# A new hand-written order for a fused attention and highway kernel, with fewer SBUF operations on VectorE

## Chip, cores and metric

The kernel runs on one core of a Trainium2 chip. The metric is device time in microseconds (us) of one execution. The engines are TensorE (PE for matmuls, PEld for its weight loads), VectorE (DVE), ScalarE (ACT), GpSimd (POOL), and SyncE (SP), which here only issues transfers (DMA). [...]

## The reference

First decayed linear attention over blocks of 64, for 4 batches, 8 heads, 768 positions and 64 columns per head; then a highway layer on the 3072 x 512 result.

```
intra = (qb @ kb.T) * lam**(i - j) for i >= j;  intra = intra @ vb
out   = intra + (qb * lam**(i + 1)) @ state
state = lam**64 * state + (kb * lam**(63 - j)).T @ vb
H = max(x @ w_h, 0);  T = sigmoid(x @ w_t + b_t);  result = T * H + (1 - T) * x
```

## The kernel before

The work is cut into 12 steps n of 256 positions, three to a batch, each with two halves b of 128 positions. A step loads k, q and v as f32 (256 KB for each half load), casts k and q to bf16 (CK, CQ), scales v by lam to a negative power (CV), transposes k and q on PE (TK, TQ in step 0; RKF, RQF, or RK, RQ in pieces of 64 rows, later) and copies them out of PSUM (EK, EQ, FK, FQ). Then come the scores (S; SA and SB with the state's matmuls laced in), the causal mask (M, DVE), the state k'v kept in PSUM (U) and copied to SBUF (KE), the product of q with the state (I), the product of masked scores with v (A), and the scaling of the result by lam to a positive power (D, DVE), which gives the transposed rows xT of the second layer. These are turned back on PE (TX, TXB) and copied to `xs` (XC).

The second layer has for each half step two FFN blocks F of four matmuls of 512 columns: F.n.b.0 with w_h into bank h, F.n.b.1 with w_t into bank t, which BP has filled with the bias. Then H = max(h, 0) - x (DVE), G = sigmoid(t) (ACT; "@S" writes it to SBUF for POOL), X = G times H (DVE or POOL), Y = X + x (DVE or POOL) and ST, the store. The last half step goes in two pieces of 256 columns (n.b.0 and n.b.1). W are the four loads of the weights (512 KB each), WC their casts.

Set-up: PW.i fills pow_o[:, i], the powers of lam for step i of a batch, with four exponentials on ACT. QB multiplies a column of ones with the bias row so that every partition has it, RB copies it to SBUF. PT loads ACT's table for the sigmoid. Z.r issues r matmuls whose result nobody reads.

The order of everything is written out in PLAN (lines 16 to 70): tokens `name.args@engine=banks`, issued from left to right, each engine working off its own tokens in that order; nothing is reordered. "Lk.0.1" loads the second half of k of step 0; tile names with a ring of buffers (BUFS, line 72) wait until the tenant before has been read. Lines that the profile names: 198 and 194 loads of k, v and q; 202 loads of W; 111 and 113 a copy or cast on ACT and on DVE or POOL; 221 CV; 233 transposes; 262 scores; 267 state; 304 M; 324 I; 335 A; 341 D; 346 PW; 378 F; 387 QB; 391 H; 396 G; 400 X; 404 Y; 408 and 412 stores; 418 Z; 437 PT.

Of the kernel before, what the change touches and what calls it, by code (L numbers as in the profile page):

```python
# [21 lines left out]
Lk.2.1 WC.1.1.0@ACT WC.1.1.1@POOL S.1.0=14 D.0.1@DVE KE.0.1@ACT WC.1.0.1@POOL Lq.3.0 BP.0.1.2@DVE=0 PT F.0.0.1.2
M.1.0.1 Lq.3.1 CV.1.2@POOL M.1.1.1 TXB.0.0=3 G.0.0.2@S F.0.1.1.2 Lk.3.1 M.1.1.0 Z.2=6 M.1.0.0 G.0.1.2@S U.1.0 Lk.3.0
WC.0.1.0@POOL A.1.1=52 BP.1.0.2@DVE=0 KE.1.0@ACT TXB.0.1=4 WC.0.1.1@POOL Lv.2.1 A.1.0 BP.1.1.2@ACT=6 I.1 CQ.2.2@DVE
XC.0.2.1@ACT U.1.1 D.1.0@DVE RQF.2=1 Lv.2.0 WC.0.0.1@ACT WC.0.0.0@POOL F.1.0.1.2 EQ.2.1@DVE XC.0.2.0@ACT D.1.1@DVE
Lv.3.0 EQ.2.0@ACT F.0.1.0.2=4 CK.2.2@DVE Lv.3.1 TXB.1.1=3 TXB.1.0=5 H.0.1.2 Lq.4.0 XC.1.2.1@ACT RKF.2=1 F.0.0.0.2=2
KE.1.1@ACT X.0.1.2@POOL EK.2.1@DVE Lq.4.1 XC.1.2.0@ACT EK.2.0@DVE S.2.0=31 G.1.0.2@S H.0.0.2 Lk.4.0 CQ.3.2@POOL
S.2.1=45 F.1.1.0.2=0 M.2.1.1 Lk.4.1 CK.3.2@ACT Y.0.1.2@POOL M.2.0.1 RQF.3=5 Lv.4.1 M.2.0.0 RKF.3=2 EQ.3.1@ACT M.2.1.0
F.1.0.0.2=4 Lq.5.0 EK.3.1@ACT CV.2.2@POOL H.1.1.2 EK.3.0@ACT S.3.1=31 Lq.5.1 H.1.0.2 EQ.3.0@ACT F.1.1.1.2 M.3.1.1
BP.2.0.2@ACT=0 Lv.4.0 CV.3.2@POOL U.2.0 M.3.0.1 S.3.0=25 Lk.5.0 KE.2.0@ACT A.2.0=14 M.3.0.0 A.2.1 I.2 Lk.5.1  # L30
CQ.4.2@ACT M.3.1.0 X.0.0.2@POOL U.3.0 D.2.0@DVE Lv.5.0 A.3.1=32 G.1.1.2 A.3.0 D.2.1@DVE RQF.4=5 KE.3.0@ACT Lv.5.1
CK.4.2@POOL F.2.0.1.2 EQ.4.0@DVE X.1.1.2@DVE Lk.6.0 I.3 Y.0.0.2@POOL G.2.0.2@S RKF.4=1 EQ.4.1@DVE Lk.6.1 D.3.0@DVE
F.2.0.0.2=4 EK.4.0@ACT D.3.1@DVE Lq.6.0 CQ.5.2@POOL EK.4.1@ACT TX.2.2=56 U.3.1 XC.2.2.0@ACT Lq.6.1 S.4.1=01
Y.1.1.2@DVE CV.4.2@POOL TXB.3.0=3 XC.2.2.1@ACT RQF.5=5 M.4.0.1 Lv.6.1 KE.3.1@ACT TXB.3.1=2 F.3.0.0.2=6 H.2.0.2
XC.3.2.0@ACT Lq.7.1 EQ.5.1@ACT M.4.1.1 CK.5.2@POOL F.2.1.0.2=0 XC.3.2.1@ACT H.3.0.2 Lv.6.0 EQ.5.0@ACT X.1.0.2@POOL
BP.3.0.2@DVE=4 SA.4=3 RKF.5=1 Lq.7.0 KE.4.0@ACT M.4.1.0 F.3.0.1.2 BP.2.1.2@ACT=6 CV.5.2@POOL EK.5.1@DVE Lk.7.0
EK.5.0@ACT H.2.1.2 SB.4=2 G.3.0.2 S.5.1=53 M.4.0.0 Lk.7.1 F.2.1.1.2 BP.3.1.2@ACT=0 M.5.1.1 Y.1.0.2@POOL Lk.8.1
KE.4.1@ACT I.4=12 M.5.0.1 CK.6.2@ACT Lk.8.0 A.4.0 SB.5=3 X.3.0.2@DVE X.2.0.2@POOL SA.5=5 G.2.1.2 A.4.1 Lv.7.0 M.5.1.0
F.3.1.1.2 CQ.6.2@ACT X.2.1.2@DVE Lv.7.1 Y.2.0.2@POOL F.3.1.0.2=5 D.4.0@DVE G.3.1.2@S Lq.9.1 KE.5.0@ACT CV.6.2@POOL
D.4.1@DVE RK.6=46 RQ.6 BP.4.1.2@ACT=0 Lq.8.1 M.5.0.0 F.4.0.0.2=1 FK.6.1@ACT H.3.1.2 Lq.8.0 FK.6.0@ACT TXB.4.0=3  # L40
FQ.6.0@DVE TXB.4.1=2 CQ.7.2@POOL XC.4.2.0@ACT F.4.1.1.2 FQ.6.1@DVE Lk.9.0 XC.4.2.1@DVE H.4.0.2 CK.7.2@POOL S.6.1=46
Lk.9.1 G.4.1.2@S SA.6=3 M.6.0.1 I.5=52 KE.6.0@ACT Y.3.0.2@POOL Lq.9.0 M.6.1.0 A.5.0 BP.4.0.2@ACT=1 SB.6=4 A.5.1
M.6.1.1 KE.6.1@ACT Lv.8.0 Y.2.1.2@POOL RQ.7=03 RK.7 D.5.1@DVE CK.8.2@ACT F.4.0.1.2 Lv.8.1 D.5.0@DVE CV.7.2@POOL
FQ.7.0@ACT TXB.5.1=6 M.6.0.0 Lv.9.1 F.4.1.0.2=2 G.4.0.2 FQ.7.1@DVE Lv.9.0 FK.7.1@ACT XC.5.2.1@DVE TXB.5.0=4
X.4.0.2@DVE RKF.8=5 FK.7.0@ACT X.3.1.2@POOL ST.0 I.6=63 XC.5.2.0@DVE EK.8.1@ACT SA.7=0 H.4.1.2 A.6.1 ST.1 EK.8.0@ACT
A.6.0 CQ.8.2@POOL S.7.1=41 M.7.1.0 KE.7.0@ACT F.5.1.0.2=5 Lq.11.1 D.6.0@DVE BP.5.0.2@ACT=2 CK.9.2@POOL Lq.11.0 RQF.8=0
# [5 lines left out]
D.7.0@DVE SA.9=6 Y.4.1.2@POOL A.8.0 Lv.11.0 BP.7.0.2@ACT=5 D.7.1@DVE F.6.1.1.2 KE.9.0@ACT X.5.1.2@POOL ST.2 M.9.1.0
CQ.10.2@ACT TXB.7.1=4 F.7.0.1.2 D.8.1@DVE ST.4 Y.5.0.2@POOL G.6.1.2@S BP.6.0.2@DVE=3 F.7.1.0.2=6 XC.7.2.1@ACT ST.3
D.8.0@DVE G.7.0.2@S Y.5.1.2@POOL TXB.7.0=4 H.7.1.2 S.9.1=21 CK.11.2@ACT SB.9=5 M.9.0.1 CK.10.2@POOL ST.5 F.6.0.1.2
BP.7.1.2@ACT=0 M.9.1.1 XC.7.2.0@ACT M.9.0.0 RK.11=26 CV.10.2@POOL G.6.0.2@S RQ.11 RQ.10=14 KE.9.1@ACT FQ.11.0@DVE
RK.10 TX.8.2=53 FQ.11.1@DVE FQ.10.1@ACT F.7.1.1.2 FK.11.1@DVE XC.8.2.1@ACT FK.11.0@DVE X.6.0.2@POOL FK.10.1@DVE
# [19 lines left out]
def kernel(  # L76
# [82 lines left out]
    for i in range(1, NST):  # L159
        P.tensor_scalar(off[:, i], in0=off[:, 0], scalar1=float(2 * C * i), scalar2=None, op0=ALU.mult)  # L160
# [183 lines left out]
    def powers(i):  # L344
        for hp in range(NP):
            A.activation(pow_o[:, i, :, hp, :], t_f, AF.Exp, scale=off[:, 0, hp:hp + 1], bias=off[:, i, hp:hp + 1] if i else 0.0)
# [39 lines left out]
    def spread(bk):  # L386
        T.matmul(bank(("qb",), bk[0], [128, DM]), lhsT=ones, rhs=b_row, start=True, stop=True)
# [9 lines left out]

    def gate(n, b, p, eng):
        y = buf("y", n, b)[:, cols(p)]
        ENG[eng].tensor_tensor(y, in0=buf("g", n, b)[:, cols(p)] if eng == "POOL" else get("t", n, b, p), in1=y, op=ALU.mult)  # L400

    def total(n, b, p, eng):
        z = cols(p)
        ENG[eng].tensor_tensor(buf("ob", n)[:, b, z], in0=buf("y", n, b)[:, z], in1=buf("xs", n)[:, b, z], op=ALU.add)  # L404
# [69 lines left out]
```

## Time and profile before

| | |
|---|---|
| runs shown | 103.04 us median of 3 (102.52 to 105.31) |
| the profiled execution | 102.99 us; span from first to last instruction 101.3 us |
| TensorE clock granted, mean | 0.987 |
| read and written | 20.97 MB, 6.29 MB |
| chain that ended last | PE 31%, DMA 29%, SP's issuing 10%, POOL 7%, DVE 7% |

The profile is one execution. A page and views of it give busy time of each engine, for the whole span or for stretches; the chain of work that ended last, followed back from the end; the timeline of an engine; and groups of instructions by line and shape. Matmuls are pipelined and their ends are modelled, so one matmul's duration is longer than the distance to the next.

### The profile page before, as it was taken

How to read it: one execution, taken by the hardware profiler on the slowest of the kernel's cores; microseconds unless marked ns; L12 is line 12 of the kernel's file. 1: busy time of each engine (PE TensorE's matmuls, PEld its weight loads, DVE VectorE, ACT ScalarE, POOL GpSimd, SP SyncE). 2: the span in 40 equal slices, each digit the busy share in tenths (PEclk: the TensorE clock that was granted, in tenths of full speed). 3: DMA queues.
4: the chain of work that ended last, by engine and by line, in shares of the span. 5: the costliest groups of instructions: out<-in, count | busy, mean ns of one | idle time of the engine just before them, and what ended most of it. 6: DMA issues, size and time to landing. Idle time of an engine off the chain costs nothing.

```text
span 101.3 us, 4242 instructions
## 1 busy us (share of the span) xinstructions
PE 91.9 (91%) x1784; PEld 57.0 (56%) x1803; DVE 85.7 (85%) x157; ACT 74.5 (74%) x134; POOL 82.3 (81%) x83
## 2 busy tenths in 40 slices
...
GB/s 22 309 300 311 357 338 365 366 340 302 254 292 306 338 300 290 299 271 304 283 288 288 319 314 395 392 310 279 294 392 364 36 6 201 6 21 366 239 307 112
DMA packets 33335, 27.54 MB, mean 272 GB/s; under 512 B 1443, under 2 KB 26275, under 8 KB 33316
## 3 DMA queue, kind: packets, MB, share of 16 engines
...
q8 instruction: 14, 0.23, 1.0%
...
q10 hardware_dynamic: 4, 0.00, 0.0%
HBM read 20.97 MB, written 6.29 MB: 269 GB/s over the span
## 4 chain that ended last, share of the span: by engine, by line
PE 31%; DMA 29%; SPq 10%; POOL 7%; DVE 7%; issue 7%; ACT 5%; DVEq 0%; POOLq 0%; ACTq 0%
DMA kf<-in_k_dram 14%; PE bt L378 9%; PE bh L378 9%; DMA w_f<-in_moe_w_h_dram 8%; DMA qf<-in_q_dram 7%; SPq L198 5%; SPq L194 4%; PE kv L267 2%; PE bs L262 2%; POOL ob L404 2%; POOL kb L113 2%; DVE y L391 2%; POOL vs L221 2%; PE bo L335 2%; SPq L202 2%
## 5 line engine op out<-in xcount | busy, mean ns | idle before, releaser
L304 DVE TENSOR_TENSOR m<-bs,tri 128x512 bf16<-128x512 f32 x48 | 31.0, 681 | 1.2 <-PE kv L267 1.0
L221 POOL TENSOR_TENSOR vs<-vf,pow_v 128x1024 bf16<-128x1024 f32 (+1 forms) x13 | 23.4, 1805 | 5.1 <-DMA vf<-in_v_dram 3.1
L378 PEld LDWEIGHTS <-xT 128*128 128x128 bf16 x200 | 17.7, 98 | 16.8 <-DVE xT L341 0.3
L404 POOL TENSOR_TENSOR ob<-y,xs 128x512 f32<-128x512 bf16 x21 | 24.3, 1173 | 0.6 <-DVE y L400 0.4
L378 PE MATMUL bh<-w_b,xT 128*128 128x512 bf16 (+1 forms) x93 | 23.8, 370 | 0.5
L378 PE MATMUL bt<-w_b,xT 128*128 128x512 bf16 (+1 forms) x89 | 23.1, 370 | 1.1 <-issue 0.3
L400 POOL TENSOR_TENSOR y<-g,y 128x512 bf16<-128x512 f32 x15 | 17.3, 1159 | 2.7 <-DVE y L391 2.6
L391 DVE SCALAR_TENSOR_TENSOR y<-bh,xs 128x512 bf16<-128x512 f32 (+1 forms) x25 | 16.3, 660 | 1.8 <-PE bh L378 1.8
L341 DVE TENSOR_TENSOR xT<-bo,pow_o 128x512 bf16<-128x512 f32 x24 | 15.6, 679 | 0.1
L111 ACT ACTIVATE ss<-kv 128x512 bf16<-128x512 f32 x19 | 11.4, 601 | 3.9 <-PE kv L267 3.8
L396 ACT ACTIVATE g<-bt 128x512 f32<-128x512 f32 x15 | 9.0, 602 | 5.0 <-PE bt L378 4.4
L111 ACT ACTIVATE bt<-b_bc 128x512 f32<-128x512 f32 (+1 forms) x20 | 11.5, 580 | 1.4 <-DVE xT L341 0.6
L262 PE MATMUL bs<-qT,kT 64*64 64x128 bf16 x384 | 11.5, 220 | 0.0
L111 ACT ACTIVATE xs<-bx 128x512 bf16<-128x512 bf16 x15 | 9.0, 604 | 1.3 <-PE bx L354 0.8
L262 PEld LDWEIGHTS <-kT 64*64 64x64 bf16 x384 | 8.2, 106 | 2.7 <-DVE kT L113 1.2
L267 PE MATMUL kv<-vs,kb 64*64 64x64 bf16 x320 | 8.6, 194 | 0.2 <-POOL vs L221 0.2
L267 PEld LDWEIGHTS <-kb 64*64 64x64 bf16 x320 | 7.0, 109 | 3.0 <-issue 2.0
L335 PE MATMUL bo<-m,vs 64*64 64x128 bf16 x384 | 8.5, 218 | 0.0
L418 PE MATMUL bspin<-blank,id 128*128 128x512 bf16 x26 | 8.3, 444 | 0.1
L113 POOL CAST kb<-kf 128x1024 bf16<-128x1024 f32 (+1 forms) x7 | 6.8, 976 | 1.5 <-DMA kf<-in_k_dram 1.5
L396 ACT ACTIVATE bt<-bt 128x512 f32<-128x512 f32 (+1 forms) x10 | 5.5, 546 | 2.4 <-PE bt L378 2.4
L335 PEld LDWEIGHTS <-vs 64*64 64x64 bf16 x384 | 6.4, 107 | 0.6
...
## 6 DMA issues: line engine op xcount, KB each, us to landing
...
```

What stands on the lines that cost most here:

```text
L111: A.activation(dst, src, AF.Copy)
L221: ENG[eng].tensor_tensor(buf("vs", n)[:, hs], in0=buf("vf", n)[:, hs].rearrange("p h (j d) -> p h j d", j=J), in1=pow_v[:, n % NST, hs, :, ...
L262: T.matmul(get("s", n, e, hp // 2)[half(b), hp % 2, j, :], lhsT=buf("kT", n)[half(e), hp, j, half(b)], rhs=q_cols(n, half(e), hp, b), star ...
L267: T.matmul(kv[half(e), hp, half(e)], lhsT=buf("kb", n)[half(b), j, 2 * hp + e, :], rhs=buf("vs", n)[half(b), 2 * hp + e, j, :], start=firs ...
L304: V.tensor_tensor(buf("m", n, e, u), in0=get("s", n, e, u), in1=tri[:, None].to_broadcast([128, 2, J, C]), op=ALU.mult)
L335: T.matmul(get("o", n, b)[half(e), hp, :], lhsT=buf("vs", n)[half(b), 2 * hp + e, j, :], rhs=buf("m", n, e, hp // 2)[half(b), hp % 2, j, : ...
L341: V.tensor_tensor(cut(buf("xT", n)[:, :, b * C:(b + 1) * C]), in0=get("o", n, b).rearrange("e k (j p) -> e k p j", j=Q), in1=cut(pow_o[:, ...
L378: T.matmul(t, lhsT=buf("xT", n)[:, j, b * C:(b + 1) * C], rhs=w_b[w][:, j, z], start=(j == 0 and not w), stop=(j == KC - 1), skip_group_ch ...
L391: V.scalar_tensor_tensor(buf("y", n, b)[:, z], in0=get("h", n, b, p), scalar=0.0, in1=buf("xs", n)[:, b, z], op0=ALU.max, op1=ALU.subtract)
L396: A.activation(buf("g", n, b)[:, cols(p)] if to == "S" else t, t, AF.Sigmoid)
L400: ENG[eng].tensor_tensor(y, in0=buf("g", n, b)[:, cols(p)] if eng == "POOL" else get("t", n, b, p), in1=y, op=ALU.mult)
L404: ENG[eng].tensor_tensor(buf("ob", n)[:, b, z], in0=buf("y", n, b)[:, z], in1=buf("xs", n)[:, b, z], op=ALU.add)
```

## The change

The order is replaced as a whole. What is different in kind:

- Behind step 0, DVE no longer casts k or q from SBUF to SBUF (CQ.1, CQ.2 and CK.2 were there), and the adds Y.1.1 and Y.8.0 go from DVE to POOL. In step 0, DVE takes over CK.0.0, CV.0.0 and PW.2.
- PW.2 is no longer four exponentials but one product of pow_o[:, 0] with `grown`, the exponential of the per-step offset.
- The bias product QB comes in two halves of 256 columns, QB.0 and QB.1.
- The loads of step 1's v go ahead of the weights, both stand ahead of all of step 2, and v of step 2 goes ahead of q and k of step 3. ST.2 and ST.3 stand among the last loads of v; before, all loads came ahead of ST.2.
- In the last two pieces, t comes ahead of h on PE, and the result is max(h, 0) g + (1 - g) x: G to SBUF, GN = sigmoid(-t) to `rest`, R = rest times x, HG = max(h, 0) times g into `part`, Y = part + rest. R, HG and Y are on DVE.
- Counts by engine: Z 31 matmuls before, 23 after; BP on DVE 5 before, 2 after; X on POOL 15 and 13, Y on POOL 21 and 23.

The head and the end of PLAN, then the functions:

```diff
-Lk.0.0 Lq.0.0 Lq.0.1 Lk.0.1 Lv.0.1 Lq.1.0 Z.9=5 Lq.1.1 PW.0@ACT CQ.0.0@DVE Lv.0.0 CK.0.0@POOL Lk.1.0 Lk.1.1
-CQ.0.1@POOL TK.0.0=2 W.1.0 PW.2@ACT Z.1=5 TQ.0.2=3 CK.0.1@DVE W.1.1 Z.1=5 TK.0.1=4 EQ.0.0@DVE QB=6 EQ.0.1@DVE Lv.1.0
-CV.0.1@POOL EK.0.0@DVE EK.0.1@ACT Lv.1.1 S.0.0=01 RB@ACT S.0.1=53 CQ.1.2@DVE Lq.2.1 Z.3=4 PW.1@ACT M.0.0.0 RQF.1=2
...
-H.10.0.2 G.10.0.2 F.11.0.0.2=1 XC.11.2.0@DVE Y.10.1.2@POOL BP.11.1.1@ACT=6 ST.9 X.10.0.2@DVE F.11.0.1.2 H.11.0.2
-Y.10.0.2@POOL F.11.1.0.0=5 G.11.0.2 TXB.11.1=3 F.11.1.1.0 X.11.0.2@DVE XC.11.2.1@ACT ST.10 F.11.1.0.1=0 G.11.1.0
-H.11.1.0 F.11.1.1.1 Y.11.0.2@POOL H.11.1.1 X.11.1.0@DVE G.11.1.1 X.11.1.1@DVE ST.11.0.2 Y.11.1.0@DVE Y.11.1.1@DVE
-ST.11.1.0 ST.11.1.1
+Lk.0.1 Lq.0.1 Lq.0.0 Lv.0.1 Lk.0.0 Lv.0.0 Z.10=5 CK.0.1@DVE Lq.1.0 PW.0@ACT Lq.1.1 CQ.0.1@POOL Lk.1.0 Lk.1.1
+CQ.0.0@DVE Lv.1.1 PW.1@ACT PW.2@DVE TQ.0.2=2 Lv.1.0 QB.0=3 Z.1=5 EQ.0.0@DVE CV.0.1@POOL W.1.0 CK.0.0@DVE TK.0.1=4
+Z.1=5 EQ.0.1@DVE PT TK.0.0=6 EK.0.1@DVE W.1.1 CV.0.0@DVE S.0.1=01 Z.2=5 W.0.1 M.0.1.1 EK.0.0@ACT U.0.0 W.0.0 S.0.0=24
+CQ.1.2@POOL QB.1 KE.0.0@ACT RB@ACT M.0.1.0 BP.0.1.2@ACT=5 Lq.2.1 U.0.1 M.0.0.0 RQF.1=6 BP.0.0.2@ACT=3 M.0.0.1 I.0=14
+Lq.2.0 CK.1.2@POOL EQ.1.0@ACT A.0.0 KE.0.1@DVE A.0.1 EQ.1.1@ACT Z.1=0 Lk.2.1 D.0.0@DVE RKF.1=2 Z.1=0 Lk.2.0 EK.1.1@ACT
+EK.1.0@DVE Z.1=1 CV.1.2@POOL D.0.1@DVE S.1.0=06 S.1.1=21 TXB.0.1=4 M.1.0.1 Lv.2.1 WC.1.0.0@ACT M.1.1.1 U.1.0
+WC.1.0.1@ACT TXB.0.0=2 M.1.0.0 Z.6=1 M.1.1.0 Lv.2.0 WC.1.1.0@ACT WC.1.1.1@POOL XC.0.2.1@DVE KE.1.0@ACT XC.0.2.0@DVE
+F.0.1.1.2 Lq.3.1 I.1=10 WC.0.1.0@POOL A.1.0 WC.0.1.1@POOL A.1.1 U.1.1 D.1.0@DVE F.0.0.1.2 Lq.3.0 WC.0.0.0@ACT
+WC.0.0.1@POOL D.1.1@DVE G.0.1.2@S TXB.1.0=6 Lk.3.1 KE.1.1@DVE F.0.0.0.2=4 G.0.0.2@S XC.1.2.0@DVE Lk.3.0 CQ.2.2@POOL
...
+D.10.0@DVE F.9.1.1.2 G.8.0.2 X.9.0.2@POOL BP.10.0.2@ACT=2 XC.10.2.1@DVE F.10.1.1.2 M.11.1.1 G.9.1.2 Y.9.0.2@POOL
+X.8.0.2@DVE A.11.1=03 G.10.1.2 A.11.0 X.9.1.2@DVE I.11 Y.8.0.2@POOL F.10.1.0.2=6 BP.11.1.1@ACT=1 D.11.0@DVE
+Y.9.1.2@POOL TXB.10.0=5 ST.8 H.10.1.2 F.10.0.0.2=0 XC.10.2.0@ACT BP.11.0.2@ACT=6 X.10.1.2@DVE F.10.0.1.2 ST.9 H.10.0.2
+Y.10.1.2@POOL F.11.0.0.2=5 D.11.1@DVE G.10.0.2 X.10.0.2@DVE TXB.11.0=4 F.11.0.1.2 XC.11.2.0@ACT BP.11.1.0@DVE=0
+Y.10.0.2@POOL H.11.0.2 TXB.11.1=3 G.11.0.2 F.11.1.1.0 F.11.1.0.0=4 XC.11.2.1@ACT X.11.0.2@DVE ST.10 F.11.1.1.1
+G.11.1.0@S GN.11.1.0 F.11.1.0.1=2 Y.11.0.2@POOL HG.11.1.0 GN.11.1.1 R.11.1.0@DVE G.11.1.1@S R.11.1.1@DVE HG.11.1.1
+ST.11.0.2 Y.11.1.0@DVE Y.11.1.1@DVE ST.11.1.0 ST.11.1.1
...
@@ -158,6 +158,8 @@
         P.tensor_copy(off[half(e), 0], ln[half(e)].rearrange("p (h e) -> p e h", e=2)[:, e])
     for i in range(1, NST):
         P.tensor_scalar(off[:, i], in0=off[:, 0], scalar1=float(2 * C * i), scalar2=None, op0=ALU.mult)
+    grown = singles.tile([128, NST, NP], F32)
+    A.activation(grown[:, 1:], off[:, 1:], AF.Exp)
     pow_o = singles.tile([128, NST, 2, NP, C], F32)
     b_bc = singles.tile([128, DM], F32)
     w_f = [singles.tile([128, KC, DM], F32, name=f"w_f{i}") for i in range(2)]
@@ -173,6 +175,9 @@
     def buf(x, *key):
         return ring[x][turn.get(x, turn["kf"])(*key) % BUFS[x]]
 
+    rest = singles.tile([C, DM], F32)
+    part = singles.tile([C, DM], F32)
+    parted = set()
     made = {}
 
...
-    def powers(i):
+    def powers(i, eng):
+        if eng != "ACT":
+            ENG[eng].tensor_tensor(pow_o[:, i], in0=pow_o[:, 0], in1=grown[:, i, None, :, None].to_broadcast([128, 2, NP, C]), op=ALU.mult)
+            return
         for hp in range(NP):
             A.activation(pow_o[:, i, :, hp, :], t_f, AF.Exp, scale=off[:, 0, hp:hp + 1], bias=off[:, i, hp:hp + 1] if i else 0.0)
 
-    def spread(bk):
-        T.matmul(bank(("qb",), bk[0], [128, DM]), lhsT=ones, rhs=b_row, start=True, stop=True)
+    def spread(p, bk):
+        t = bank(("qb",), bk[0] if bk else 0, [128, DM])
+        T.matmul(t[:, cols(p)], lhsT=ones, rhs=b_row[:, cols(p)], start=p == 0, stop=True, skip_group_check=True)
 
@@ -395,13 +404,27 @@
         t = get("t", n, b, p)
         A.activation(buf("g", n, b)[:, cols(p)] if to == "S" else t, t, AF.Sigmoid)
 
+    def sigm_rest(n, b, p):
+        A.activation(rest[:, cols(p)], get("t", n, b, p), AF.Sigmoid, scale=-1.0)
+
+    def kept(n, b, p, eng):
+        z = cols(p)
+        ENG[eng].tensor_tensor(rest[:, z], in0=rest[:, z], in1=buf("xs", n)[:, b, z], op=ALU.mult)
+
+    def gated(n, b, p):
+        z = cols(p)
+        V.scalar_tensor_tensor(part[:, z], in0=get("h", n, b, p), scalar=0.0, in1=buf("g", n, b)[:, z], op0=ALU.max, op1=ALU.mult)
+        parted.add((n, b, p))
+
     def gate(n, b, p, eng):
         y = buf("y", n, b)[:, cols(p)]
         ENG[eng].tensor_tensor(y, in0=buf("g", n, b)[:, cols(p)] if eng == "POOL" else get("t", n, b, p), in1=y, op=ALU.mult)
 
     def total(n, b, p, eng):
         z = cols(p)
-        ENG[eng].tensor_tensor(buf("ob", n)[:, b, z], in0=buf("y", n, b)[:, z], in1=buf("xs", n)[:, b, z], op=ALU.add)
+        last = (n, b, p) in parted
+        ENG[eng].tensor_tensor(buf("ob", n)[:, b, z], in0=part[:, z] if last else buf("y", n, b)[:, z],
+                               in1=rest[:, z] if last else buf("xs", n)[:, b, z], op=ALU.add)
```

More of the change, by code (lines that the diff above doesn't have):

```diff
@@ L22 @@
[L22 to L46, printed above, removed]
@@ L52 @@
[L52 to L56, printed above, removed]
```

57 lines of the change are left out of this document (39 added, 18 removed).

## The prediction

> **What bounds the kernel now.** I read the page's busy line first, then the view that cuts the span into stretches, then the chain of waits in order of time, then the timeline of each engine at the two ends. Busy times first, then four stretches: before the first useful matmul, to 30.06 us, to 95 us, the rest. The columns of the stretches are length, busy us of PE, PEld, DVE, ACT and POOL, granted clock, DMA share and GB/s.
>
> ```profile
> PE 91.9 (91%) x1784; PEld 57.0 (56%) x1803; DVE 85.7 (85%) x157; ACT 74.5 (74%) x134; POOL 82.3 (81%) x83
> 0.00:6.72 6.72, 5.48 (x15) 2.07 (x16) 2.18 (x6) 4.01 (x9) 4.31 (x18) 1.00 0.64 192
> 6.72:30.06 23.34, 22.24 (x379) 13.67 (x382) 18.69 (x34) 18.18 (x33) 13.48 (x15) 1.00 1.08 327
> 30.06:95.00 64.94, 62.58 (x1380) 40.09 (x1395) 62.02 (x111) 50.86 (x91) 62.69 (x51) 1.00 0.87 266
> 95.00:101.30 6.30, 1.59 (x17) 1.20 (x14) 2.85 (x7) 1.48 (x4) 1.77 (x2) 0.79 0.59 212
> ```
>
> From 30.06 to 95 us PE is idle for only 64.94 - 62.58 = 2.36 us, and what it does there is useful work, because both orders place all idle-filling matmuls (Z) in steps 0 and 1. DVE (62.02) and POOL (62.69) have as little room; ACT has 14 us. So the long middle can give back at most 2.36 us. Before 30.06 it is otherwise: 22.24 us count as busy, but much of that is Z and waiting, and DMA is full (1.08 at 327 GB/s). What an order can win is what PE has finished by 30 us, when data no longer set the pace. The chain shows where PE stands then.
>
> ```profile
> 28.23 0.62 PE bktr L233 x8
> 28.85 0.86 PE bh L378 x4
> 29.72 0.35 PE bs L262 x16
> 30.06 0.97 PE bt L378 x4
> 31.03 0.30 PE kv L267 x12
> 33.08 0.45 PE bo L335 x30
> ```
>
> These are RKF.3, F.1.0, half of S.3, the last FFN block of step 1 (F.1.1.1), U.2 and A.3. They also give my units: F 0.86, U about 0.4, A 0.45, S 0.45. Eight transposes are 0.45: the 0.62 holds the last one's run-out, and F began 0.62 after the first.
>
> **Step by step: the first 30 us.** The arrival of the data decides. Rows of the timeline: start, duration, engine, operation, and in brackets idle time and releaser.
>
> ```profile
> 12.23 1.04 POOL L113 CAST kb<-kf 128x1024 bf16<-128x1024 f32 x1 [0.78 <-DMA kf<-in_k_dram]
> 14.91 1.18 POOL L113 CAST w_b<-w_f 128x512 bf16<-128x512 f32 x2 [0.78 <-DMA w_f<-in_moe_w_t_dram]
> 16.71 1.91 POOL L221 TENSOR_TENSOR vs<-vf,pow_v 128x1024 bf16<-128x1024 f32 x1 [0.62 <-DMA vf<-in_v_dram]
> 21.43 0.62 POOL L113 CAST w_b<-w_f 128x512 bf16<-128x512 f32 x1 [0.94 <-DMA w_f<-in_moe_w_h_dram]
> 23.25 0.69 DVE L113 CAST kb<-kf 128x1024 bf16<-128x1024 f32 x1 [0.36 <-DMA kf<-in_k_dram]
> 27.12 1.06 ACT L111 ACTIVATE kb<-kf 128x1024 bf16<-128x1024 f32 x1 [1.22 <-DMA kf<-in_k_dram]
> 28.82 3.76 POOL L221 TENSOR_TENSOR vs<-vf,pow_v 128x1024 bf16<-128x1024 f32 x2 [0.94 <-DMA vf<-in_v_dram]
> 15.54 1.28 DVE L341 TENSOR_TENSOR xT<-bo,pow_o 128x512 bf16<-128x512 f32 x2
> 16.28 0.82 PE L378 MATMUL bt<-w_b,xT 128*128 128x512 bf16 x3 [0.17 <-DVE xT L341]
> 16.55 1.28 ACT L437 ACT_TABLE_LOAD   x1
> ```
>
> Count SP's loads in pieces of 256 KB (a W is two). The rows tie positions to times: the 10th piece is in at 12.23, the 14th at 14.91, the 16th at 16.71, the 22nd at 21.43, the 24th at 23.25, the 28th at 27.12, the 30th at 28.82: 0.83 us each ((28.82 - 12.23) / 20). The new order of SP gives other tenants: v of step 1 now precedes the weights, so w_t is complete with piece 16 (16.71, not 14.91); w_h with piece 20 (about 20.1, not 21.43); q of step 2 with 22 (21.43), k with 24 (23.25, as before), v of step 2 with 26 (about 25, not 28.82), q of step 3 with 28, k of step 3 with 30 (28.82, not 27.12).
>
> Step 0 in the new order: the costs are these (two rows of the timeline, three of the groups by line with mean ns behind the busy time, one more of the timeline).
>
> ```profile
> 4.41 3.67 ACT L346 ACTIVATE pow_o<-t_f,off 128x256 f32<-128x256 f32 x8
> 4.47 0.42 POOL L160 TENSOR_SCALAR off<-off 128x4 f32<-128x4 f32 x2
> L387 PE MATMUL bqb<-b_row,ones 1*128 1x512 f32 x2 | 1.1, 640 | 0.0
> L304 DVE TENSOR_TENSOR m<-bs,tri 128x512 bf16<-128x512 f32 x48 | 31.0, 681 | 1.2 <-PE kv L267 1.0
> L221 POOL TENSOR_TENSOR vs<-vf,pow_v 128x1024 bf16<-128x1024 f32 x11 | 21.3, 1943 | 2.8 <-DMA vf<-in_v_dram 1.9 <-DVE m L304 0.5 <-DMA qf<-in_q_dram 0.4
> 26.20 2.47 DVE L304 TENSOR_TENSOR m<-bs,tri 128x512 bf16<-128x512 f32 x4
> ```
>
> Four masks take 2.47, so each further full DVE operation costs (2.47 - 0.68) / 3 = 0.60. PW.2 leaves ACT (four of 3.67 / 8 = 0.46, 1.8 us less) for one DVE product of 128x1024. No row shows it: below, a DVE cast of this size is 0.69; above, POOL's two-source product is 1.94. I take 1.2, two masks, the row nearest in kind. CV.0.0 on DVE is likewise one mask, 0.6, between 0.35 (half the cast) and 0.97 (half POOL's product). The exponential `grown` has 8 columns where pow_o has 256 and costs at most its 0.46, but ACT now waits for POOL's `off`, done at 4.89; so PW.0 starts near 5.2 instead of 4.41 and ends at 7.0, PW.1 ends at 8.9, and the table load (1.28), moved here from 16.55, at 10.2. Only then comes EK.0.0, 0.46 or more: S.0.0 starts near 11. DVE meanwhile runs from the arrival of q's second half, the third piece (12.23 - 7 x 0.83 = 6.4): casts and copies of half a step CQ, EQ, CK, EQ, EK at most 0.4 each (a little over half of 0.69), PW.2 1.2, CV 0.6, four masks 2.4, KE 0.6: 6.8, so D.0.0 starts at 13.2, or 13.7 to 14.1 with waits for S.0.0 and for POOL; now it is 15.54. The two bias halves are half of 1.1 each: nothing in sum, only one half moved behind S.0.0.
>
> The gain of 1.5 us in D.0.0 is not kept: the first F needs w_t, in at 16.71, cast by 17.4, so F starts at 17.5 instead of 16.28. From there I add PE's list in units: all eight F, I.1, A.1, U.1, TXB.1, RQF.2, RKF.2, S.2, RQF.3, U.2, A.2. It waits 0.4 for k of step 2 (POOL's or ACT's cast is 1.06) and 0.3 for q of step 3, and reaches RKF.3 at 29.95. At 30.06 the new PE has F.1.1.1 (0.86), U.2 (0.4) and A.2 (0.45) done beyond what it has now, and lacks half of S.3 (0.23) and most of RKF.3 (0.35). **PE is 1.1 us ahead.** Bounds: no gain where v of step 2 comes no sooner than now, and 1.7 if RKF.3 is not late.
>
> **The middle.** From the masks of step 1 on DVE loses two BP and a half, two casts, two adds, and gains two KE and two small copies: by rows 1.6 us less. POOL loses two gates and a cast for two adds, ACT takes three BP, three casts and the like, 4.5 us, of 14 free. Of the copies behind step 0 (CQ.1, CQ.2, CK.2) the last ran at 23.25, when POOL had ended its cast of 21.43 and next had X.0.1, whose H stood behind CK.2 on DVE: it held up nothing. What did collide are the two adds on DVE.
>
> ```profile
> 35.84 1.04 POOL L113 CAST qb<-qf 128x1024 bf16<-128x1024 f32 x1
> 36.59 0.84 DVE L404 TENSOR_TENSOR ob<-y,xs 128x512 f32<-128x512 bf16 x1
> 36.84 2.35 POOL L221 TENSOR_TENSOR vs<-vf,pow_v 128x1024 bf16<-128x1024 f32 x1
> 88.84 1.29 DVE L404 TENSOR_TENSOR ob<-y,xs 128x512 f32<-128x512 bf16 x1
> 89.67 1.49 POOL L404 TENSOR_TENSOR ob<-y,xs 128x512 f32<-128x512 bf16 x1
> ```
>
> The DVE add lasts longer the longer POOL was already at work, and the POOL operation queued behind ends late by 2.35 - 1.94 = 0.41 and 1.49 - 1.15 = 0.34 (the add of the tail's rows): one waits for the other to end. Both adds go to POOL. But PE, not they, is full here, so I credit a quarter of its 2.36 idle: **-0.6**; ends -2.36 (all gone) and +0.8 (a third more idle, from ACT's 4.5 us).
>
> **The tail.** Rows of the timeline from the last gates on.
>
> ```profile
> 95.28 0.69 DVE L400 TENSOR_TENSOR y<-bt,y 128x512 bf16<-128x512 f32 x1 [0.29 <-ACT bt L396]
> 95.32 0.60 ACT L111 ACTIVATE xs<-bx 128x512 bf16<-128x512 bf16 x1
> 95.95 0.76 DVE L391 SCALAR_TENSOR_TENSOR y<-bh,xs 128x256 bf16<-128x256 f32 x2
> 95.99 0.60 PE L378 MATMUL bt<-w_b,xT 128*128 128x256 bf16 x4
> 96.05 1.15 POOL L404 TENSOR_TENSOR ob<-y,xs 128x512 f32<-128x512 bf16 x1 [0.42 <-DVE y L400]
> 96.62 0.83 DVE L400 TENSOR_TENSOR y<-bt,y 128x256 bf16<-128x256 f32 x2
> 96.63 0.37 ACT L396 ACTIVATE bt<-bt 128x256 f32<-128x256 f32 x1 [0.44 <-PE bt L378]
> 97.37 0.75 DVE L404 TENSOR_TENSOR ob<-y,xs 128x256 f32<-128x256 bf16 x2
> ```
>
> DVE is busy without a break from 95.28 to 98.12: X, then six half pieces. New: X, HG, R, R, HG, Y, Y, again six, each 0.36 behind the last and 0.42 long. ACT has four sigmoids of 0.37 for two, behind XC: 95.7, 96.05, 96.4, 96.75 to 97.1. HG.0 runs at 96.1. R reads `rest` and `xs`, both in SBUF, as the colliding adds did, and POOL has Y.11.0 running from 96.05 to 97.2. If R waits for that: R 97.2, R, HG, Y, Y end at 97.2 + 4 x 0.36 + 0.42 = 99.06, **+0.9**. If not, the six end at 96.1 + 5 x 0.36 + 0.42 = 98.3, +0.2. I take +0.9, since both collisions above show such a wait. [...]
>
> **Sum.** The profiled execution took 102.99 us, 1.69 beyond its span of 101.30. 102.99 - 1.1 - 0.6 + 0.9 = **102.2 us**. The median of the runs shown is 103.04, as good as the same, so nothing is added.
>
> **Rivals.**
>
> *Faster: the middle gives too.* DVE and POOL are each 95% busy from 30 us and lose about 1.6 us each, so most of PE's 2.36 idle (say 1.8) may vanish with its cause, the early lead may be 1.5, and R may start ahead of Y.11.0 (tail +0.2): 102.99 - 1.5 - 1.8 + 0.2 = 99.9. For it: the stretches' DVE and POOL columns. Against it: PE's own column, and ACT gets 4.5 us more.
>
> *Slower: the weights come too late.* Place: first F at 17.5, not 16.28. If v of step 2 buys PE nothing, because its F of steps 0 and 1 are still waiting and RQF.3 and RKF.3 (k of step 3 one piece pair later, 1.7 us) become the wait at 30 us, PE is 1.2 to 1.7 us behind instead of 1.1 ahead, and the middle, full, cannot make it up: 102.99 + 1.5 + 0.9 = 105.4. It decides once fewer than seven F are done when RQF.3 starts. For it: DMA is full to 30 us. Against it: the unit count, which has eight.
>
> *The change does not do what it says:* a cast off DVE frees nobody, as at 23.25; then the early lead alone stands against the tail: 102.99 - 1.1 + 0.9 = 102.8, inside the forecast.
>
> **How the numbers follow.** A measurement of this kernel can tell about 2%, 2.1 us, from no change. Forecast with the case that only the early lead counts: 0.54, 101 to 104.5; faster rival 0.29, 99 to 101; slower rival 0.17, 104.5 to 106. The range, from 99.6 to 105.0, leaves about a tenth on each side. Chances: faster by over 2% (below 100.9) 0.29, within 0.55, slower (above 105.1) 0.16.
>
> **What would show it.** The first F near 17.5 and D.0.0 near 14; A.2 done by 30 us; PE idle of under 2 us between 30 and 95; no DVE operation beyond 0.7 us in the middle; R starting when POOL's last add ends, and the last DVE add about 2.5 us behind the last matmul (now 98.12 - 96.59 = 1.5). The prediction is wrong if D.0.0 is later than 15.5, if a load waits long in SP's queue (ST.2 and ST.3 now stand ahead of the last v loads), or if the middle's idle of PE grows beyond 3 us.

## The result and the profile after

| | before | after |
|---|---|---|
| median of 20 runs each | 103.03 us (101.56 to 105.31) | 103.84 us (102.99 to 105.61) |
| ratio (of the runs named below) | | 1.0111, 95% interval 1.0072 to 1.0151 |
| profiled execution, span | 102.99 us, 101.3 us | 104.04 us, 102.3 us |

The new order is slower by about 1%. That is inside the range given and within 2%, but forecast was a small gain. Ratios, here and below, compare only executions that lie within 1.5% of the fastest of their kernel, so they can differ from the quotient of the medians.

The busy line of the page after the change, then the stretches (length, busy us of PE, PEld, DVE, ACT and POOL, granted clock, DMA share, GB/s):

```profile
PE 93.1 (91%) x1801; PEld 57.3 (56%) x1801; DVE 86.1 (84%) x158; ACT 77.1 (75%) x137; POOL 79.1 (77%) x79
6.72:30.06 23.34, 22.08 (x354) 13.31 (x352) 18.84 (x35) 16.86 (x29) 14.38 (x14) 1.00 1.06 350
30.06:95.00 64.94, 63.41 (x1418) 40.16 (x1417) 61.20 (x110) 54.70 (x95) 58.64 (x48) 1.00 0.82 264
95.00:102.30 7.30, 2.11 (x21) 1.67 (x19) 4.15 (x8) 2.19 (x6) 1.94 (x2) 0.82 0.38 144
```

PE's idle time in the middle fell from 2.36 to 64.94 - 63.41 = 1.53 us, DVE (62.02 to 61.20) and POOL (62.69 to 58.64) lost work, as forecast, DVE half of the 1.6 us. The loss shows first at the two ends. First the timeline of the early stage (start, duration, engine, operation, in brackets idle time and releaser):

```profile
14.01 0.68 DVE L346 TENSOR_TENSOR xT<-bo,pow_o 128x512 bf16<-128x512 f32 x1
17.98 1.46 PE L441 MATMUL bspin<-blank,id 128*128 128x512 bf16 x6 [0.21 <-DVE m L309]
19.27 1.03 PE L386 MATMUL bt<-w_b,xT 128*128 128x512 bf16 x4
31.38 0.62 PE L238 MATMUL bktr<-id,kb 128*128 128x128 bf16 x8
```

D.0.0 starts at 14.01, as forecast. But the first F starts at 19.27 and not at 17.5: in front of it in PE's own order stands Z.6, six matmuls whose result nobody reads, into bank 1. (By the plans the order before has 27 such matmuls, not 31, and the new one 23.) That bank frees only when a mask of step 1 has read it, so the six could not fill an idle time; they ran when F could have. RKF.3 comes at 31.38 where 29.95 was forecast.

The end, same view: the last matmul block, POOL's last add, and DVE's last pieces.

```profile
96.51 0.60 PE L386 MATMUL bh<-w_b,xT 128*128 128x256 bf16 x4
96.57 1.15 POOL L426 TENSOR_TENSOR ob<-y,xs 128x512 f32<-128x512 bf16 x1 [0.78 <-DVE y L421]
96.91 1.42 DVE L412 TENSOR_TENSOR rest<-rest,xs 128x256 f32<-128x256 f32 x2
98.26 0.41 DVE L416 SCALAR_TENSOR_TENSOR part<-bh,g 128x256 f32<-128x256 f32 x1
98.59 0.74 DVE L426 TENSOR_TENSOR ob<-part,rest 128x256 f32<-128x256 f32 x2
```

The last matmul ends at 97.11 (96.59 before), the last DVE add at 99.33, 2.22 behind it (1.53 before). From there to the end of the span are about 3.0 us (about 3.2 before). So the span's +1.0 is 0.52 by the last matmul, 0.69 behind it, and about 0.2 given back between the last add and the end.

### The profile page after: what moved, and what is told of

Its sections match the earlier page's. It is cut to its first block, busy times and chain, and to the rows that moved or that the text cites. A ratio compares the mean times of both kernels' runs of the same rounds, so it can differ in the third digit from the quotient of the medians.

```text
span 102.3 us, 4269 instructions
## 1 busy us (share of the span) xinstructions
PE 93.1 (91%) x1801; PEld 57.3 (56%) x1801; DVE 86.1 (84%) x158; ACT 77.1 (75%) x137; POOL 79.1 (77%) x79
## 4 chain that ended last, share of the span: by engine, by line
PE 62%; DVE 21%; ACT 8%; issue 5%; DVEq 0%
PE bt L386 16%; PE bh L386 13%; DVE m L309 7%; PE bspin L441 6%; PE bs L267 6%; PE bo L340 4%; DVE y L400 4%; PE kv L272 3%; PE bo L329 3%; DVE xT L346 2%; PE bx L362 2%; PE bqtr L238 2%; ACT qT L111 2%; ACT kT L111 2%; DVE kT L113 2%
## 5 line engine op out<-in xcount | busy, mean ns | idle before, releaser
L426 POOL TENSOR_TENSOR ob<-y,xs 128x512 f32<-128x512 bf16 x23 | 26.4, 1159 | 3.1 <-DVE y L421 2.9
L386 PE MATMUL bt<-w_b,xT 128*128 128x512 bf16 (+1 forms) x100 | 24.6, 371 | 0.0
L226 POOL TENSOR_TENSOR vs<-vf,pow_v 128x1024 bf16<-128x1024 f32 (+1 forms) x12 | 22.3, 1865 | 2.6 <-DMA vf<-in_v_dram 2.6
L421 POOL TENSOR_TENSOR y<-g,y 128x512 bf16<-128x512 f32 x13 | 15.0, 1161 | 6.8 <-DVE y L400 3.6
L400 DVE SCALAR_TENSOR_TENSOR y<-bh,xs 128x512 bf16<-128x512 f32 x23 | 15.5, 683 | 1.2 <-PE bh L386 1.0
L111 ACT ACTIVATE bt<-b_bc 128x512 f32<-128x512 f32 (+1 forms) x23 | 13.3, 591 | 2.0 <-DVE xT L346 1.1
L267 PE MATMUL bs<-qT,kT 64*64 64x128 bf16 x384 | 12.2, 219 | 1.8 <-ACT w_b L111 0.8
L111 ACT ACTIVATE ss<-kv 128x512 bf16<-128x512 f32 x17 | 10.2, 599 | 2.1 <-PE kv L272 2.0
L405 ACT ACTIVATE g<-bt 128x512 f32<-128x512 f32 (+1 forms) x15 | 8.6, 572 | 2.9 <-PE bt L386 2.6
L267 PEld LDWEIGHTS <-kT 64*64 64x64 bf16 x384 | 8.4, 106 | 3.9 <-DVE kT L113 1.8
L272 PE MATMUL kv<-vs,kb 64*64 64x64 bf16 x320 | 9.1, 194 | 0.0
L272 PEld LDWEIGHTS <-kb 64*64 64x64 bf16 x320 | 7.0, 109 | 2.8 <-issue 2.1
L405 ACT ACTIVATE bt<-bt 128x512 f32<-128x512 f32 x10 | 5.8, 581 | 2.2 <-PE bt L386 2.2
L111 ACT ACTIVATE qb<-qf 128x1024 bf16<-128x1024 f32 x7 | 7.4, 1055 | 0.0
```

Of the source, the lines that this page charges most:

```text
L111: A.activation(dst, src, AF.Copy)
L226: ENG[eng].tensor_tensor(buf("vs", n)[:, hs], in0=buf("vf", n)[:, hs].rearrange("p h (j d) -> p h j d", j=J), in1=pow_v[:, n % NST, hs, :, ...
L267: T.matmul(get("s", n, e, hp // 2)[half(b), hp % 2, j, :], lhsT=buf("kT", n)[half(e), hp, j, half(b)], rhs=q_cols(n, half(e), hp, b), star ...
L272: T.matmul(kv[half(e), hp, half(e)], lhsT=buf("kb", n)[half(b), j, 2 * hp + e, :], rhs=buf("vs", n)[half(b), 2 * hp + e, j, :], start=firs ...
L386: T.matmul(t, lhsT=buf("xT", n)[:, j, b * C:(b + 1) * C], rhs=w_b[w][:, j, z], start=(j == 0 and not w), stop=(j == KC - 1), skip_group_ch ...
L400: V.scalar_tensor_tensor(buf("y", n, b)[:, z], in0=get("h", n, b, p), scalar=0.0, in1=buf("xs", n)[:, b, z], op0=ALU.max, op1=ALU.subtract)
```

## The experiments

Theories before the runs: (Z) the early term is lost to Z.6; (A) the end is longer because R waits for POOL's Y.11.0; (B) the end is longer because of the new form itself, with more operations. A third question came out of the first four runs and is told below.

**Without Z.6.**

```diff
-... M.1.0.0 Z.6=1 M.1.1.0 Lv.2.0 ...
+... M.1.0.0 M.1.1.0 Lv.2.0 ...
```

> The new kernel without the six filling matmuls Z.6 that stand ahead of its first FFN block. Theory A (they are on PE's path: they wait for a mask of step 1 to release their bank, run 17.98 to 19.4 us, and F follows at 19.27 though its weights were cast at 17.5): first F at 17.5 to 17.8 us, PE's last matmul 1.2 to 1.6 us earlier than 97.11, time 1.2 to 1.6 us below the new kernel's 103.84, about 102.4. Rival B (the arrival of q, k of steps 2 and 3 and DVE's masks take the lead back): first F at 17.5 to 17.8, but the last matmul less than 0.4 us earlier, time 103.4 to 103.9. Rival C (PE's clock drops in the gap): the matmuls behind it stand 0.43 us apart instead of 0.215, and the time is above 103.84.

Median 103.61 us (6 runs; before 103.55 on that chip), ratio 1.0016 (0.9927 to 1.0105). Three rows of PE's timeline:

```profile
17.60 1.03 PE L386 MATMUL bt<-w_b,xT 128*128 128x512 bf16 x4
30.07 0.62 PE L238 MATMUL bktr<-id,kb 128*128 128x128 bf16 x8
94.24 0.60 PE L386 MATMUL bh<-w_b,xT 128*128 128x256 bf16 x4
```

F starts at 17.60 and RKF.3 at 30.07: both as forecast, and Z.6 alone cost 31.38 - 30.07 = 1.31 us. The granted clock was 1.00 from 6.72 to 95 us in this profile, so rival C falls. (The profiles below agree, but for those with an early fall of the clock: RKF.3 starts at 29.86 to 30.07 in the seven without Z.6, at 31.38 to 31.63 in the three with it.) In this profile, the shortest of its six executions (101.78 us), the last matmul ends at 94.84, 1.75 ahead of before; the prediction's first two terms were -1.1 and -0.6. That compares a short execution with a middling one of before, whose shortest on this chip took 101.58 us; the medians show no lead.

**More of the same: Z.18 for Z.6.**

```diff
-... M.1.0.0 Z.6=1 M.1.1.0 ...
+... M.1.0.0 Z.18=1 M.1.1.0 ...
```

> The new kernel with eighteen filling matmuls ahead of its first FFN block instead of six (twelve more of 0.215 us: 2.6 us). Theory A (they stand on PE's path and nothing later makes up for a late PE): first F at 21.8 to 21.9 us, the time 2.2 to 2.6 us above the new kernel: 106.0 to 106.5. Rival B (data or DVE's masks set the pace behind them): first F as late, but the time less than 1.0 us above 103.84.

Median 106.56 us (6 runs; before 103.12), ratio 1.0405 (1.0286 to 1.0523). The profile is of an execution in which the clock fell early (two of the six were such); a stretch with that, and two rows of PE:

```profile
15.00:19.00 4.00, 3.70 (x48) 2.16 (x46) 1.17 (x3) 2.39 (x6) 1.56 (x3) 0.55 1.06 392
21.02 4.05 PE L441 MATMUL bspin<-blank,id 128*128 128x512 bf16 x18 [0.21 <-DVE m L309]
24.90 1.03 PE L386 MATMUL bt<-w_b,xT 128*128 128x512 bf16 x4
```

The first F starts 24.90 - 21.02 = 3.88 us behind the first Z (1.29 with six): the fillers stand in the way one for one. The other four runs, at a mean clock of 0.98 or more, took 105.38 to 106.94, on average 2.3 us above after's median, for twelve more fillers of 0.215 us (2.6). So a delay ahead of the first F reaches the end of the kernel.

**The end in the old form.** The last two pieces as before, with t kept ahead of h:

```diff
-G.11.1.0@S GN.11.1.0 F.11.1.0.1=2 Y.11.0.2@POOL HG.11.1.0 GN.11.1.1 R.11.1.0@DVE G.11.1.1@S R.11.1.1@DVE HG.11.1.1
+G.11.1.0 F.11.1.0.1=2 Y.11.0.2@POOL H.11.1.0 X.11.1.0@DVE G.11.1.1 H.11.1.1 X.11.1.1@DVE
```

> The new order, but the last two pieces as before: G times (relu(h) - x), plus x. Theory A (the tail is lengthened because R waits for POOL's add Y.11.0): the last DVE add ends 1.5 to 1.6 us behind the last matmul instead of 2.22, time 0.6 to 0.7 us below the new kernel's 103.84, about 103.2. Rival B (the order of t ahead of h, or ACT, lengthens it): the gap stays above 2.0 us and the time within 0.2 us of 103.84.

Median 104.07 us (6 runs), ratio 1.0143 (1.0066 to 1.0220): no gain in the time. Yet behind the last matmul are 1.76 us instead of 2.22 (and 1.53 where h is ahead of t, below). Timeline, last matmul block and last adds, and one row of the middle:

```profile
97.17 0.60 PE L386 MATMUL bh<-w_b,xT 128*128 128x256 bf16 x4
98.78 0.75 DVE L426 TENSOR_TENSOR ob<-y,xs 128x256 f32<-128x256 bf16 x2
46.65 0.22 PE L272 MATMUL kv<-vs,kb 64*64 64x64 bf16 x2 [1.52 <-issue]
```

What it gained at the end it had lost before the last matmul (97.77 against 97.11), most of it at 46.65: PE stood still for 1.52 us, waiting for nothing that the profile shows ("issue"). This was in none of my theories.

**Both undone.** Without Z.6, and with this old form.

> Both: the new order without Z.6 and with the last two pieces as before. If both theories A hold and add up, 1.8 to 2.3 us below the new kernel: 101.6 to 102.0, that is about 1% faster than the kernel before. If the early lead is taken back (rival B of the first), 103.0 to 103.3, the same as before.

Median 103.53 us (6 runs; before 103.55), ratio 0.9957 (0.9866 to 1.0048). Level with before; span 100.4, one stand-still of 0.45 us at 77.25.

**The new end alone, on the order before.** Only the last two lines of the plan and the functions HG, GN and R.

> The kernel before with only the last two pieces changed: t ahead of h on PE, and relu(h) g + (1 - g) x. Theory A: R waits for POOL's add Y.11.0, the last DVE add 2.2 to 2.5 us behind the last matmul instead of 1.53, time 0.6 to 0.9 us above 103.03: about 103.8. Rival B (no wait, the products only move): within 0.2 us of 103.03.

Median 104.28 us (6 runs), ratio 1.0051 (0.9942 to 1.0160): the time does not settle it. The timeline does:

```profile
98.44 0.60 PE L381 MATMUL bh<-w_b,xT 128*128 128x256 bf16 x4
98.49 1.15 POOL L420 TENSOR_TENSOR ob<-y,xs 128x512 f32<-128x512 bf16 x1 [0.43 <-DVE y L415]
98.98 1.27 DVE L406 TENSOR_TENSOR rest<-rest,xs 128x256 f32<-128x256 f32 x2
100.52 0.74 DVE L420 TENSOR_TENSOR ob<-part,rest 128x256 f32<-128x256 f32 x2
```

Again 100.52 + 0.74 - 99.04 = 2.22 us behind the last matmul, in another order, with the two R beside POOL's add.

**Without POOL's last add.** Y.11.0 is left out.

```diff
-... F.11.1.0.1=2 Y.11.0.2@POOL HG.11.1.0 ...
+... F.11.1.0.1=2 HG.11.1.0 ...
```

> The new kernel without POOL's last add (Y.11.0 is left out, so the half step before the last one is stored unfinished). Theory A (R on DVE waits for this add on POOL to end): the two R take 0.75 to 0.8 us together instead of 1.42, and the last DVE add ends 1.5 to 1.6 us behind the last matmul instead of 2.22. Rival B (R waits for ACT's sigmoids): R takes 1.3 us or more and the gap stays above 2.1 us.

```profile
97.38 0.60 PE L386 MATMUL bh<-w_b,xT 128*128 128x256 bf16 x4
97.78 0.75 DVE L412 TENSOR_TENSOR rest<-rest,xs 128x256 f32<-128x256 f32 x2
98.78 0.75 DVE L426 TENSOR_TENSOR ob<-part,rest 128x256 f32<-128x256 f32 x2
68.38 0.21 PE L267 MATMUL bs<-qT,kT 64*64 64x128 bf16 x1 [1.68 <-issue]
```

The two R take 0.75 instead of 1.42 us, and 1.55 us stand behind the last matmul. Theory A is shown, B falls: the new form is no longer by itself, and no shorter either (1.53 before). Median 102.87 us (12 runs), ratio 1.0049 (0.9990 to 1.0107), again with a stand-still of PE, 1.68 us at 68.38.

**Without Z.6, the end as before** (h ahead of t, too).

> The new order without Z.6 and with the end of the kernel before: h ahead of t on PE, G times (relu(h) - x), plus x. Theory A: first F at 17.6 us, last matmul near 95.2 us, last DVE add 1.5 us behind it, so 1.3 to 1.9 us below the new kernel: 102.0 to 102.5, about 1% faster than the kernel before. Rival B (the middle of the new order is worse than that of before): 102.9 to 103.5.

Median 103.39 us (6 runs; before 103.12), ratio 1.0134 (1.0020 to 1.0248). Behind the last matmul 1.53 us, first F at 17.60: both losses are out, and still it is no faster than before. It has two stand-stills:

```profile
44.97 0.22 PE L271 MATMUL kv<-vs,kb 64*64 64x64 bf16 x2 [1.27 <-issue]
67.30 0.21 PE L266 MATMUL bs<-qT,kT 64*64 64x128 bf16 x1 [0.80 <-issue]
```

**The two colliding adds alone.** Kernel before, with Y.1.1 and Y.8.0 on POOL: the reason that I gave for the middle.

```diff
-Y.1.1.2@DVE ... Y.8.0.2@DVE
+Y.1.1.2@POOL ... Y.8.0.2@POOL
```

> The kernel before with its two adds in the middle, Y.1.1 and Y.8.0, on POOL instead of DVE; nothing else changes. Theory A (the two collisions cost PE nothing, because PE is full): no DVE operation above 0.76 us between 30 and 95 us, and the time within 0.3 us of 103.03. Rival B (the prediction's middle term, -0.6 us, comes from them): 102.2 to 102.6.

Median 103.17 us (6 runs; before 103.12), ratio 1.0112 (1.0013 to 1.0212). No gain, though the collisions are gone (no DVE operation of the middle is above 0.7 us): what they cost DVE and POOL does not reach the end.

**What the stand-stills are.** In several kernels they come in the middle of the laced small matmuls SA.5 (45 us) and SA.8 (67 us), two smaller ones near 78 us, and not in every execution. The page has a DMA queue of the kind "instruction", q8, with 14 packets, 0.23 MB in a run, so about 16 KB each; I call them blocks, and that they hold PE's instructions is at first an assumption. Theory F: PE has used up its instructions and waits for a late block. Rival P: these places stand still by themselves. The stores of steps 0 to 8 can be made smaller without changing a wait in front of them; in the new order this was done without Z.6 and with the end as before:

```diff
+p = 16 if n < 9 else C
-... out[i:i + 2 * C].rearrange("(b p) f -> p b f", p=C), in_=buf("ob", n))
+... out[i:i + 2 * C].rearrange("(b p) f -> p b f", p=C)[:p], in_=buf("ob", n)[:p])
```

> The new order without Z.6 and with the end as before (as in the run where PE stood still for 1.27 us at 44.97 and 0.80 us at 67.30, waiting for nothing that the profile shows), and of the stores ST.0 to ST.8 only 16 of 128 rows are written: 4.1 MB of the 27.5 MB of transfers are left out. Theory F (PE waits for its own next instructions, which come by the same 16 DMA engines and stand behind data): no stand-still over 0.3 us between 40 and 75 us is left, and the late instruction blocks are gone; the time falls by 1 to 2 us, to 101.5 to 102.5. Rival P (the places are set by the program, dense small matmuls, whatever the DMA does): a stand-still of 0.8 us or more at about 45 or 67 us remains.

> The kernel before with only 16 of 128 rows of ST.0 to ST.8 written. It is the control: what fewer bytes do by themselves in the order before, whose profile has one stand-still of PE of 0.50 us. Theory F: it gains less than the new order does from the same cut, at most 1 us (102 to 103). If both gain the same, to 0.3 us, the late instruction blocks do not set the two orders apart.

> A second look at the new order with 16 of 128 rows of ST.0 to ST.8 written, whose first profile had no stand-still over 0.3 us. Theory F with late blocks made by the traffic: again none at 45 to 70 us. If one of 0.8 us or more is there, the first look was chance, and the stores are not what makes the block late.

New order 101.92 us (4 runs), ratio 0.9885 (0.9805 to 0.9964); order before 102.20 us (4 runs), ratio 0.9906 (0.9823 to 0.9990). Against before, both are about 1 us faster. But the new order must be held against its own version with all stores, 1.0134 (median 103.39): by the ratios it gains 2.5 us and the order before 1.0, by the medians 1.5 and 1.0. Theory F expects this sign, but the intervals are too wide to show it. The two profiles of the new order show no stand-still over 0.3 us:

```profile
65.24 0.21 PE L266 MATMUL bs<-qT,kT 64*64 64x128 bf16 x1 [0.25 <-issue]
```

while the order before kept one of 0.51 us at 72.43. Two executions are few, since three of nine with all stores had none over 0.5 either; that the traffic makes the block late is not shown.

The version with both undone was run again, as the candidate, and profiled a second and a third time:

> The new order without Z.6 and with the old form of the last two pieces (t ahead of h kept): the version that was fastest against the kernel before so far (0.9957, from 0.9866 to 1.0048), in more runs. My account by terms: early -1.1 as first predicted, middle 0, end +0.2, so 0.9 us under the kernel before, ratio 0.991. Rival (the new order has no lead that lasts to the end): ratio 1.000 or over.

> A third look at the version without the two moves (stand-stills of 0.45 us at 77 in the first profile, of 1.51 and 1.07 us at 45 and 68 in the second). Theory F: the stand-still comes where a block of instructions starts to move after PE has issued 1360 of its instructions, and ends 1.1 to 1.4 us after the block has landed; span 100 to 101 without, 102 to 103 with both. Rival: stand-stills without a late block.

Median 103.75 us (6 runs; before 103.18): no lead. The second and the third profile of this one kernel, two rows each:

```profile
45.34 0.22 PE L272 MATMUL kv<-vs,kb 64*64 64x64 bf16 x2 [1.51 <-issue]
68.33 0.21 PE L267 MATMUL bs<-qT,kT 64*64 64x128 bf16 x1 [1.07 <-issue]
```

```profile
45.30 0.22 PE L272 MATMUL kv<-vs,kb 64*64 64x64 bf16 x2 [1.50 <-issue]
67.30 0.21 PE L267 MATMUL bs<-qT,kT 64*64 64x128 bf16 x1 [0.48 <-issue]
```

Spans 102.6 and 101.6 against 100.4 in the first profile: 2.2 and 1.2 us more, with 2.13 and 1.53 us more of stand-still (0.45 in the first). Now the blocks. In the view of the DMA queues, the block that matters for the first place starts to move between 42.75 and 43.00 us in the third profile, and in the first, which hardly stood still there, already between 41.25 and 41.50 (packets, MB, share of the DMA engines in that quarter microsecond):

```profile
q8 instruction: 1, 0.02, 26.7%
```

```profile
q8 instruction: 1, 0.02, 25.1%
```

The table has, for each profile of the new order, how many weight loads PE had begun when that block started to move. (Weight loads are counted because matmul records can be missing: the first two profiles of both undone have 1795 weight loads each, but 1774 and 1795 matmuls.)

| profile | weight loads begun | stand-still at SA.5, us |
|---|---|---|
| Z.18 | 645 | 0 |
| few stores, second and first profile | 652, 658 | 0, 0 |
| after | 655 | 0 |
| without POOL's add | 664 | 0 |
| both undone, first profile; without Z.6 | 667, 668 | 0.1, 0.1 |
| both undone, third profile | 675 | 1.50 |
| end as before | 681 | 1.27 |
| both undone, second profile | 689 | 1.51 |
| old form of the end | 693 | 1.52 |

Late block, stand-still; no late block, none, with nothing between. All 14 stand-stills of 0.36 us or more that the profiles put down to "issue", of both orders, end 1.2 to 1.5 us after a block has landed.

The traces show more. Number the weight loads of a run: the 14 end at load 734 (four of them), 1245 (six) and 1501 (two) in the new order, with Z.6 or without, and at 1118 and 1374 (one each) in the order before. To within one, these are whole multiples of 128 apart, and 14 blocks for 1801 weight loads are 129 to a block. So in all 14 PE stood at a border between blocks, at scores, state, products with v and turned rows alike. And over the 13 borders of each of the 17 profiles, taken every 128 loads from these, PE passed none sooner than 1.2 us after its block had landed. Theory F is shown; that the blocks are PE's rests on this agreement, as no row of the profile names their owner. With two more that the profile puts down to ACT (below) there are 16 such stand-stills of 0.36 us or more on the 221 borders, the longest of 1.68 us.

The test by an edit: move work in front of the two places, on PE alone.

```diff
-A.4.1 M.5.1.1 Lq.8.1 SA.5=5 CQ.6.2@ACT SB.5=6 I.4 M.5.0.1
+A.4.1 M.5.1.1 Lq.8.1 I.4 SA.5=5 CQ.6.2@ACT SB.5=6 M.5.0.1
-CV.9.2@POOL SA.8=4 FK.9.1@DVE FK.9.0@ACT TXB.7.1=5 M.8.1.0 F.6.1.1.2
+CV.9.2@POOL F.6.1.1.2 SA.8=4 FK.9.1@DVE FK.9.0@ACT TXB.7.1=5 M.8.1.0
```

> The new order without Z.6 and with the old form of the last two pieces, and two moves on PE alone: I.4 (8 matmuls, 0.45 us) goes ahead of SA.5 and SB.5, and the FFN block F.6.1.1 (0.86 us) ahead of SA.8 instead of behind TXB.7.1. Both stand in front of the two stretches of small matmuls in which PE stood still at 45 and 67 us. Theory F (the stand-still is a block of PE's own instructions that lands too late): each place gains the time of what was put ahead of it, so 1.51 and 1.07 us shrink to about 1.1 and 0.2 or less, and the time to 102.5 to 103 against 103.75 without the moves. Rival P (these instructions stand still by themselves): the same stand-still, 0.8 us or more, later by the time of what was moved ahead.

> A second look at the kernel with the two moves. Theory F: as the first, at most 1.1 us at the first place, 0.2 at the second. Rival P: 0.8 us or more at both.

Median 102.65 us (13 runs; before 103.64 in 17), ratio 0.9956 (0.9905 to 1.0007). The second profile has no stand-still over 0.3 us at either place, though the block for SA.8 started as late as in the third profile of the candidate (load 1174; 1173 there, where PE stood still for 0.48). The first profile, of an execution with a fall of the clock like that of Z.18, had both blocks late:

```profile
47.32 0.24 PE L267 MATMUL bs<-qT,kT 64*64 64x128 bf16 x2 [0.58 <-ACT g L405]
70.13 0.22 PE L272 MATMUL kv<-vs,kb 64*64 64x64 bf16 x2 [0.73 <-issue]
```

With its block at load 675, as in the third profile of the candidate, the first place stood still for 0.58 instead of 1.50 us (put down to ACT, but at load 734 and 1.2 us after the block landed, like the others). At the second, a block at 1217 gave 0.73, where one at 1215 gave 1.68 (without POOL's add). Work in front shrinks it, by 0.9 and 0.95 for 0.45 and 0.86 put there: F's direction, though the first more than its size. Rival P (0.8 or more at both places) is refuted by both profiles, and by the instructions: at load 734 a score (L267) now waits, where the state (L272) did, and at 1245 the other way round. In the time no gain of the moves is shown: their median lies 1.0 us below before's on that chip, that of the candidate 0.02 below and 0.57 above, but the ratios, 0.9956 and 0.9957, are the same. Whether either beats before stays open; both intervals reach 1.

## Why the prediction was wrong

*The early term, -1.1: failed, and it is the step that failed.* "From there I add PE's list in units" left one token of that list out, Z.6, and the first F went in at 17.5 on the weights alone. In its place the runs show 1.31 us for Z.6 (31.38 against 30.07), and the lead at 30 us becomes a lag of about 0.2 (-1.1 + 1.3). The times of the step held: D.0.0 at 14.01, F at 17.60 and RKF.3 at 30.07 (forecast 29.95) once Z.6 is out. Its size was too high even so. By 40 us the new order without Z.6 has begun one block F, a quarter of an S and 16 matmuls of U more than before's profile, and eight transposes of q and four of x fewer (by the weight loads begun). By the prediction's units that is a lead of 0.5 to 0.7 us, and with Z.6, where F and U are level and half an S is missing as well, a lag of 0.9; both are estimates.

*The middle, -0.6: not in the time.* In the one execution without Z.6 there is such a gain, the rest of the 1.75 us at the last matmul; after lost it. From RKF.3 to the last matmul after takes 97.11 - 31.38 = 65.73 us, without Z.6 94.84 - 30.07 = 64.77, and the difference of 0.96 is nearly the two stand-stills of after:

```profile
66.82 0.21 PE L267 MATMUL bs<-qT,kT 64*64 64x128 bf16 x1 [0.36 <-issue]
78.61 0.55 PE L340 MATMUL bo<-m,vs 64*64 64x128 bf16 x25 [0.53 <-issue]
```

Of this I had nothing: "quarter of its 2.36 idle" took PE's idle time for waits on DVE and POOL that fall with their work. DVE and POOL did have less to do, and other waits came: over the nine profiles of the new order with all stores and without the two moves, stand-stills of "issue" sum to 11.2 us, 1.2 us on average; in three profiles of the order before (itself, the new end, the two adds) there is one, of 0.50:

```profile
61.69 0.38 PE L363 MATMUL bx<-id,xT 64*128 64x64 bf16 x14 [0.50 <-issue]
```

A second one there, with the two adds on POOL, the profile puts down to ACT, whose copy had ended at 78.53:

```profile
79.11 0.41 PE L262 MATMUL bs<-qT,kT 64*64 64x128 bf16 x14 [1.22 <-ACT ss L111]
```

It stands at load 1501, to within one, and 1.4 us after a block landed. So the order before is not free of them: 0.6 us on average against 1.2. Three profiles and nine are few, and how much of the difference in the median comes from here is not measured. The reason that I gave, the two colliding adds, brings nothing by itself (1.0112, not under 1).

*The end, +0.9: right in mechanism, +0.69 in size.* R waits for POOL's add; without it the pair takes 0.75 for 1.42. The size was a little high: the two R ended 98.33 - 97.72 = 0.61 behind POOL's add, where two full ones (0.78) were counted; about 0.2 given back behind the last add was not in the sum.

*The sum.* For the profiled execution: -1.75 (both terms, as in the one execution without Z.6) + 1.31 (Z.6) + 0.96 (mostly stand-stills) + 0.69 - 0.2 = +1.0, as the spans differ by 102.3 - 101.3. This splits a difference between single executions and must come out; it is no check, and the -1.75 holds for one short execution. The rival that is nearest is not the one of late weights, which came on time, but "does not do what it says": some single executions show the order's lead, the medians do not. That the time fell inside the range given is luck: neither of the two gains forecast is in the median. And two of the signs set for being wrong did not come: D.0.0 is ahead of 15.5, and the middle's idle stays below 3 us. Both concern parts that held, and neither what stands ahead of F.
